# Attention and MLP on one core: weighed values in place of bias rows, batch 0 in row strips, a new written-out order

## The chip, the cores and the metric

One core of a Trainium2 chip runs the whole program. The metric is the time of one launch on the device, in microseconds (us); lower is better. The engines are named as the profile names them: PE (TensorE, matmuls), PEld (its weight loads), DVE (VectorE), ACT (ScalarE), POOL (GpSimd), SP (SyncE, which only issues DMAs here). DMAs issued from POOL go by the queue q0 (software descriptors, and only this queue can change the type on the way); DMAs issued from SP go by q1 and the one from ACT by q10 (hardware descriptors). All of them end on the same 16 DMA engines.

## What is computed

```python
B, H, S, D = 8, 8, 576, 64                  # batches, heads, tokens, head width
scores = q @ k.T / sqrt(D)                  # causal
cum    = cumsum(max(s, 0), axis=-1)         # the gate's running sum
scores = scores + min(cum[key] - cum[query], 0)
attn   = softmax(scores)                    # over the keys up to the query
x      = concat_heads(attn @ v)             # (8, 576, 512)
xn     = (x - mean) / sqrt(var + 1e-6) * g_ln
out    = x + max(xn @ w_ch1, 0) @ w_ch2     # 512 -> 2048 -> 512
```

All inputs and the output are float32 in device memory. Within a row of the softmax the query's own term of the gate cancels, so what matters of the gate is a factor exp(cum[key]) on each key. There are two ways to bring it in: as a term of the score (a bias), or as a factor on the key's row of v and on the one that counts for the softmax's denominator.

## The kernel before, in words

576 tokens are four tiles of 128 and a last one of 64. Each batch needs its k and q with the head width on the partitions (a transpose), scores with keys on the partitions, exp on ACT, the product with v on PE (for each head and query tile, `exp(scores)` is the stationary operand and v the moving one, with a column of ones for the denominator), a normalisation on DVE, the layer norm (DVE, with one power on POOL), and the MLP: 16 groups of hidden units (`mlp1`, four matmuls of 512 columns each, then a relu on ACT or DVE) and four token tiles of output (`mlp2`, 16 matmuls of 512 columns each, then an add on DVE and a DMA to memory). The 64-token ends of the batches are gathered two by two in a ninth, mixed MLP chunk.

Three kinds of batches are treated differently before the change:

- Batch 0 goes token tile by token tile, so that the work can begin when the first 128 tokens have landed. `ld_cast_tile` (L178) loads k and q of a tile with a change to bf16 on the way. The gate is put in as four bias rows: the running sum is scanned on DVE (`cum_scan`, L291), split into three bf16 pieces on DVE and ACT, transposed on PE (`bias_tr`, L271) and copied beside k and q, so that each head has 68 rows. `tile_tr` (L943) transposes every head by itself (8 transposes for each tile and group of four heads), `tile_scores` (L965) makes the scores of one head at a time from 68 rows, with a mask matmul (`L978`) on each diagonal block, and `tile_pv` (L1016) multiplies with v.
- Batch 1 uses bias rows too. Its k and q come pair of heads by pair (`ld_cast`, L181), where a partition holds six tokens of a head in a row, are transposed with `tr_kind` (L317), and go head by head through `scores` (L382), `scores_d` (L420), `pv` (L573) and `pv_norm` (L592).
- Batches 2 to 7 have no bias. POOL multiplies v and the ones with the weights exp(...) (`weigh_v` L229, `weigh_ones` L239). Two heads lie on the two halves of the partitions (64 rows each), and one `burst` (L541) sends the matmuls of both alternately to the two halves of the array. Six exps (`burst_exp`), four masks on POOL (`burst_mask`), then `pv_two` (L613) and `norm_two` (L639) for each head, `tails` (L514) for the last 64 keys of all heads. Batch 2's k and q come pair by pair like batch 1's, are copied on ACT (`side_two` L342), transposed on PE (`tr_two` L355) and copied back (`evac_two` L365). Batches 3 to 7 come as f32 rows by SP (`ld_rows` L211), are cast on POOL (`cast_rows`) and transposed by DMA (`tr_rows` L221).

The order of the work on every engine is written out by hand as words in a string, `PLAN` (L1278), and each word calls one function (`STEPS`, L1195). Each engine takes its instructions strictly in that order. The words used below are: `S`, `x`, `V`, `N` for scores, exp, product with v and normalisation of a tile of batch 0; `M` and `r` for pieces of batch 0's `mlp1` and their relu; `B2.n`, `bx`, `bm`, `Y`, `K` for burst, exp, mask, product and normalisation of the pair n (four pairs to a batch, so `B2.8` is the first burst of batch 2); `sd` for the tails; `u` and `U` for the next unit of the MLP queue, which holds the batches in turn; `vm` and `vo` for the weighing; `lr`, `lv` for f32 loads by SP; `la` and `l` for the layer norm's output and `D`, `Da` for its transpose by DMA.

POOL issues the loads that change the type among its other work. SP issues its DMAs in order, and a DMA of SP that waits for a buffer or for a result holds up those behind it.

Of the kernel before, what the change touches and what calls it, by code (L numbers as in the profile page):

```python
# [9 lines left out]
F32 = mybir.dt.float32  # L10
# [6 lines left out]
P = 128  # L17
# [13 lines left out]
def fast_path(  # L31
# [24 lines left out]
    KA = D + 4  # L56
# [5 lines left out]
    NOLD = 2  # L62
    NPAIR = 3
    N0 = 12
    D2 = D + 2
    ET = H * TL + 2 * TL
    NM = 10
    KT = 96
    QT = 6
    QP = S // QT  # L70

# [7 lines left out]
    early = ctx.enter_context(ExitStack())  # L79
    pairs = early.enter_context(tc.tile_pool(name="pairs", bufs=4))  # L80
    ps = ctx.enter_context(ExitStack())
    pool = {
        tag: ps.enter_context(
            tc.tile_pool(name="ps_" + tag, bufs=n, space=bass.MemoryType.PSUM)
        )
        for tag, n in (("m", 2), ("s", 3), ("t", 2), ("o", 1))
# [18 lines left out]
    eight = hT[0:BH, 0, 0 : 2 * P].bitcast(F32)  # L105
# [5 lines left out]

    def home(gam):
        return 2 if gam == 2 else gam % 2
# [11 lines left out]
    c3f = const.tile([P, 3 * S], BF16, name="c3")  # L125
    c3 = c3f[0:KT].rearrange("p (j s) -> p j s", j=3)
    ed = [c3f[:, i * ET : (i + 1) * ET] for i in range(2)]
    c_hi, c_mid, c_lo = (c3[0:BH, j, :] for j in range(3))
    zeros = hT[:, 1, :]

    rowb = const.tile([P, NT, 2 * H, KA], BF16, name="rowb")

    rows = [
        x[:, 0 : NT * 2 * H * D].rearrange("p (t u h d) -> p t u h d", t=NT, u=2, h=H)
        for x in (rowb.rearrange("p t h c -> p (t h c)"), kqf[2])
    ]

# [10 lines left out]
    ready = {}  # L148


    def pair_src(kind, g):
        src = k if kind == "k" else q
        b, j = g // 4, g % 4
        return src[b, 2 * j : 2 * j + 2].rearrange("h (p t) d -> p h (t d)", t=QT)

    def pair_tile(kind):
        return pairs.tile([P, 2, QT * D], BF16, name=kind + "p", tag=kind + "p")


    def tile_src(kind, t):  # L160
        pn = P if t < NF else TL
        src = k if kind == "k" else q
        return src[0, :, t * P : t * P + pn, :].rearrange("h s d -> s h d")

    def tile_dst(kind, t):
        pn = P if t < NF else TL
        u = "kq".index(kind)
        return rowb[0:pn, t, u * H : (u + 1) * H, 0:D]

    def ld_tile(kind, t, eng):  # L170
        tmp = stage.tile([P, H, D], F32, name="tiletmp", tag="st")
        eng.dma_start(out=tmp, in_=tile_src(kind, t))
        loaded[kind, t] = tmp

    def cast_tile(kind, t, eng):
        copy_on(eng, tile_dst(kind, t), loaded.pop((kind, t)))

    def ld_cast_tile(kind, t):  # L178
        nc.gpsimd.dma_start(out=tile_dst(kind, t), in_=tile_src(kind, t))  # L179
# [5 lines left out]
    def ld_cast_pair(g):  # L185
        ld_cast("k", g)
        ld_cast("q", g)

    def ld_cast_v(b, t):
        pn = P if t < NF else TL  # L190
        nc.gpsimd.dma_start(  # L191
            out=v_bf[b % 2][:pn, t, :, 0:D],
            in_=v[b, :, t * P : t * P + pn, :].rearrange("h s d -> s h d"),
        )
# [4 lines left out]
    src_of = {"k": k, "q": q, "v": v}  # L199

    def ld_f32(kind, b, t):
        pn = pn_of(t)
        own = kind == "v" and "v" in pool
        tmp = (pool["v"] if own else stage).tile([P, H, D], F32, name="rowtmp", tag="st")
# [4 lines left out]
        loaded[kind, b, t] = tmp  # L209

# [4 lines left out]
    def cast_rows(b, t, u):  # L215
        pn = pn_of(t)
        nc.gpsimd.tensor_copy(  # L217
            out=rows[b % 2][0:pn, t, u], in_=loaded.pop(("kq"[u], b, t))[0:pn]
        )
# [1356 lines left out]
```

## Time and profile before

| | us |
|---|---|
| three runs | 346.12, 345.09, 346.25 (median 346.12) |
| the profiled execution | 345.24 |
| its span, first to last instruction | 343.7 |
| PE busy | 333.9 (97%) |
| DVE busy | 207.1 (60%) |
| ACT busy | 186.8 (54%) |
| POOL busy | 168.7 (49%) |

The span of the profile runs from the first to the last instruction; 1.54 us of the execution's time lie around it. "Busy" is the time in which at least one instruction of the engine was under way. A matmul is under way far longer than it holds up the next one, so the price of a matmul on PE is read from start to start and not from its duration. A row of the timeline gives the start, the length, the engine, the line of the kernel, what is written and read, and how many neighbours of the same kind were merged into the row; in square brackets stands how long the engine had been idle before, and who released it. A row of a table by windows gives the stretch, its length, the busy time of PE, PEld, DVE, ACT and POOL with the number of instructions, the granted clock, the share of the DMA engines and GB/s. A row of a DMA queue gives the packets, MB (as written), and the time of the packets as a share of the 16 engines; the shares can pass 100% because packets of one engine overlap.

### The profile page before, as it was taken

The page shows a single profiled execution, that of the slowest core. Times are in us where ns is not written, and L with a number is a line of the kernel's source. Part 1 is how long each engine was busy: PE and PEld are TensorE (multiplying, and loading weights), DVE is VectorE, ACT ScalarE, POOL GpSimd, SP SyncE. Part 2 cuts the span into 40 slices and gives each one's busy share as a digit, 9 for nine tenths or more (in the row PEclk, how much of TensorE's full clock was granted, in tenths as well). Part 3 has the DMA queues.
Part 4 walks back from the last instruction along what each step waited for, and adds up shares of the span by engine and source line. Part 5 has one row for each costly group of instructions (what it writes and reads, how often), then busy time and mean ns, then how long its engine had stood idle before and what let it go on. Part 6 is the DMA issues. An engine that isn't in the chain of part 4 may idle for free.

```text
span 343.7 us, 8035 instructions
## 1 busy us (share of the span) xinstructions
PE 333.9 (97%) x3093; PEld 185.4 (54%) x3093; DVE 207.1 (60%) x589; ACT 186.8 (54%) x347; POOL 168.7 (49%) x306
## 2 busy tenths in 40 slices
PE   7999999899999999999999999999999999999994
PEld 2989765445545555555455555554555444444443
DVE  7688787937675787545753774557448624523412
ACT  4888899668755685448546864386344204202200
POOL 8997678876588766755684476441301001000000
PEclk9999999999999999999999999999999999999998
DMA  9999999799999999997687955600410141021022
GB/s 153 189 184 179 201 198 212 174 243 225 198 220 248 220 226 202 212 229 157 154 198 194 224 106 126 138 2 2 122 63 0 29 126 46 2 79 44 0 64 65
DMA packets 147962, 48.59 MB, mean 141 GB/s; under 512 B 135280, under 2 KB 143760, under 8 KB 147920
## 3 DMA queue, kind: packets, MB, share of 16 engines
q1 hardware_dynamic: 121856, 38.34, 51.4%
q0 software_dynamic: 24304, 8.92, 22.1%
q10 hardware_dynamic: 1760, 0.79, 0.9%
q8 instruction: 25, 0.41, 0.5%
q14 instruction: 17, 0.14, 0.1%
HBM read 37.11 MB, written 9.44 MB: 135 GB/s over the span
## 4 chain that ended last, share of the span: by engine, by line
PE 85%; POOL 7%; DVE 2%; DMA 2%; issue 1%; POOLq 0%
PE py L780 35%; PE ph L761 34%; PE pot L627 7%; DMA v_bf<-in_v_dram 2%; POOL v_bf L191 2%; PE sa L548 2%; POOL rowb L179 2%; PE sc L548 1%; PE sb L548 1%; PE pot L583 1%; DVE xn L710 1%; POOL w_bf L252 1%; POOL kq L910 1%; DVE yo L792 0%; DVE stats L669 0%
## 5 line engine op out<-in xcount | busy, mean ns | idle before, releaser
L780 PE MATMUL py<-w_bf,hT 128*128 128x512 bf16 (+2 forms) x608 | 130.9, 368 | 1.1 <-DVE yo L792 1.1
L761 PE MATMUL ph<-xT,w_bf 128*128 128x512 bf16 x480 | 109.8, 379 | 0.0
L752 ACT ACTIVATE hT<-ph 128x512 bf16<-128x512 f32 x102 | 61.2, 604 | 80.4 <-PE ph L761 78.8
L780 PEld LDWEIGHTS <-hT 128*128 128x128 bf16 x608 | 56.0, 98 | 61.4 <-issue 1.4
L761 PEld LDWEIGHTS <-w_bf 128*128 128x128 bf16 x544 | 51.0, 98 | 56.2
L492 POOL TENSOR_SCALAR_AFFINE_SELECT er<-er 128x256 bf16<-128x256 bf16 x96 | 37.5, 405 | 60.2 <-ACT er L553 45.1
L792 DVE SCALAR_TENSOR_TENSOR yo<-py,rstd,xb 128x512 f32<-128x512 f32 x32 | 24.0, 750 | 47.5 <-PE py L780 43.8
L553 ACT ACTIVATE er<-sb 128x512 bf16<-128x512 f32 x48 | 28.2, 609 | 21.7 <-PE sb L548 18.5
L750 DVE TENSOR_SCALAR hT<-ph 128x512 bf16<-128x512 f32 x34 | 23.4, 690 | 25.3 <-PE ph L761 24.6
L553 ACT ACTIVATE er<-sa 128x512 bf16<-128x512 f32 x48 | 28.6, 609 | 13.1 <-PE sa L548 10.2
L232 POOL TENSOR_TENSOR v_bf<-rowtmp,wt 128x512 bf16<-128x512 f32 (+1 forms) x30 | 33.8, 1134 | 2.8 <-DMA rowtmp<-in_v_dram 2.7
L553 ACT ACTIVATE er<-sc 128x512 bf16<-128x512 f32 x48 | 28.8, 613 | 5.4 <-PE sc L548 5.4
L627 PEld LDWEIGHTS <-er 128*128 128x128 bf16 x672 | 25.7, 97 | 9.5 <-issue 0.6
L627 PE MATMUL pot<-v_bf,er 128*128 128x66 bf16 x672 | 28.0, 193 | 0.0
L710 DVE SCALAR_TENSOR_TENSOR xn<-xb,mv,gb 128x512 bf16<-128x512 f32 x28 | 26.9, 960 | 1.0
L684 POOL TENSOR_TENSOR rstd<-rstd,mhalf 128x4 f32<-128x4 f32 (+1 forms) x8 | 8.8, 1094 | 36.9 <-DVE rstd L683 32.6
L644 DVE TENSOR_REDUCE sums<-pot 128x5 f32<-128x10 f32 x48 | 7.9, 165 | 30.0 <-PE pot L627 29.7
L669 DVE BATCH_NORM_STATS2 stats<-xb 128x6 f32<-128x128 f32 (+1 forms) x84 | 24.0, 323 | 0.4
L217 POOL CAST kq<-rowtmp 128x512 bf16<-128x512 f32 (+1 forms) x30 | 20.0, 681 | 6.3 <-DMA rowtmp<-in_k_dram 6.2
L647 DVE TENSOR_TENSOR xb<-pot,rinvs 128x256 f32<-128x256 f32 x48 | 20.4, 424 | 1.6
L548 PEld LDWEIGHTS <-kq 64*128 64x128 bf16 x360 | 11.2, 94 | 10.1 <-issue 4.7
L987 ACT ACTIVATE er<-st 128x512 bf16<-128x512 f32 x24 | 13.1, 603 | 1.8 <-PE st L978 1.8
(173 smaller groups left out, 398.3 us busy)
## 6 DMA issues: line engine op xcount, KB each, us to landing
out_dram<-yo SPq DMA_DIRECT2D x32, 256.0 KB
rowtmp<-in_v_dram SPq DMA_DIRECT2D x24, 256.0 KB
rowtmp<-in_k_dram SPq DMA_DIRECT2D x20, 256.0 KB
rowtmp<-in_q_dram SPq DMA_DIRECT2D x20, 256.0 KB
w_bf<-in_moe_w_ch_dram POOLq DMA_DIRECT2D x8, 512.0 KB, 9.2
kp<-in_k_dram POOLq DMA_DIRECT2D x8, 144.0 KB, 8.9
qp<-in_q_dram POOLq DMA_DIRECT2D x8, 144.0 KB, 8.9
v_bf<-in_v_dram POOLq DMA_DIRECT2D x8, 128.0 KB, 8.0
```

The costliest lines, as they stand in the source:

```text
L232: e.tensor_tensor(out=v_bf[b % 2][0:pn, t, :, 0:D], in0=loaded.pop(("v", b, t))[0:pn], in1=wt[0:pn, t, b, :].unsqueeze(2).to_broadcast([pn ...
L492: nc.gpsimd.affine_select(out=out, in_=out, compare_op=ALU.is_ge, fill=0.0, base=0, pattern=pattern, channel_multiplier=-1,)
L548: nc.tensor.matmul(a, lhsT=lhsT, rhs=rhs, start=True, stop=True)
L553: nc.scalar.activation(out=er[:, 2 * n % 4 + i, o : o + 512], in_=bank["B", n].pop((name, i)), func=ACT.Exp, scale=scale,)
L627: nc.tensor.matmul(pot[:, t, :], lhsT=cols, rhs=v_bf[b % 2][:, kb, h, :], start=(kb == 0), stop=(kb == t),)
L669: nc.vector.bn_stats(out=st[b][:, t, part, :], in_=x_tiles(b)[t][:, lo:hi])
L710: nc.vector.scalar_tensor_tensor(out=xn, in0=tiles[t], scalar=mvs[b][:, t, 0:1] if b > 0 else mean0[:, t : t + 1], in1=gb, op0=ALU.subtrac ...
L750: nc.vector.tensor_scalar_max(out=dst, in0=ph, scalar1=0.0)
L752: nc.scalar.activation(out=dst, in_=ph, func=ACT.Relu)
L761: nc.tensor.matmul(ph, lhsT=w1_bf[:, kd, fb * P : (fb + 1) * P], rhs=xT[:, :, kd, :], start=(kd == 0), stop=(kd == KD - 1),)
L780: nc.tensor.matmul(py[t], lhsT=hT[:, fb, t * P : (t + 1) * P], rhs=w2_bf[:, fb, c0:c1], start=(fb == 0), stop=(fb == FB - 1),)
L792: nc.vector.scalar_tensor_tensor(out=yo, in0=py[t], scalar=rs, in1=x[:, c0:c1], op0=ALU.mult, op1=ALU.add)
```

## The change

1. The bias rows go, and with them everything that makes them: the three pieces, their transposes and copies, the small DMAs of `aug`, the memsets of constant rows. All eight batches weigh v and the ones, so batches 0 and 1 need the weights first: load of the whole gate, relu, two scans, `wr`, `wT`, `wx` now stand at the start of the plan, and v of batches 0 and 1 comes as f32 by SP and is weighed on DVE or POOL.
2. k and q of batches 0, 1 and 2 come token tile by token tile in bf16 (`ld_cast_rows`: one run of 64 values for each token and head), are transposed two heads at a time on PE (`rows_tr`, eight transposes for each tile of a batch) and copied once (`rows_evac`). The loads pair by pair, `side_two`, `tr_two`, `evac_two`, `tr_kind`, `evac_half` are gone.
3. Batch 0's scores go in row strips: two heads alternate on the two halves of the array, and one mask matmul covers several diagonal blocks of a bank.
4. Batch 1 goes by bursts like the batches after it, with masks on POOL and tails.
5. All of batch 0's `mlp1` goes in pieces of one token tile (`M`, 16 pieces of 16 matmuls of 128 columns; before, eight pieces and eight units of 512 columns). Its `mlp2` goes in named quarters `Z.t.q`.
6. PSUM: four banks for scores and two for transposes at first, six for scores after `to`.
7. The plan is new from its start to about the middle and shifted a little behind that; memsets and loads that stood ahead of it are words of it now.

The core of the diff:

```diff
-    def ld_cast(kind, g):
-        ready[kind, g] = pair_tile(kind)
-        nc.gpsimd.dma_start(out=ready[kind, g][0:QP], in_=pair_src(kind, g))
+    def ld_cast_rows(b, t, u):
+        pn = pn_of(t)
+        nc.gpsimd.dma_start(
+            out=rows_of(b)[0:pn, t, u],
+            in_=(k, q)[u][b, :, t * P : t * P + pn, :].rearrange("h s d -> s h d"),
+        )
+
+    def rows_tr(b, t):
+        pn = pn_of(t)
+        tr = ptile("s" if new[0] else "t", [P, 2, NJ, P], "trp", BF16)
+        for u in range(2):
+            for j in range(NJ):
+                nc.tensor.transpose(
+                    tr[:, u, j, 0:pn],
+                    rows_of(b)[0:pn, t, u, 2 * j : 2 * j + 2].rearrange("p h d -> p (h d)"),
+                    ident[0:pn, 0:pn],
+                )
+        bank["P", b, t] = tr
...
-    def tile_scores(t, g, i):
-        a = ptile("s", [P, 512], "st")
-        for c in range(4 if t < NF else 8):
...
+    def tile_scores(t, c):
+        w = pn_of(t)
+        n = 512 // w
+        banks = [ptile("s", [P, 512], f"st{i}") for i in range(2)]
+        blocks = [divmod(n * c + x, min(t + 1, NF)) for x in range(n)]
+        diag = [x for x in range(n) if blocks[x][1] == t]
+        for i in range(2):
+            if diag:
+                nc.tensor.matmul(
+                    banks[i].rearrange("p (x s) -> p x s", s=w)[:, diag[0] :: t + 1],
+                    lhsT=ident,
+                    rhs=maskT.unsqueeze(1).to_broadcast([P, len(diag), P]),
+                    start=True,
+                    stop=False,
+                )
+        for x in diag + [x for x in range(n) if x not in diag]:
+            j, kb = blocks[x]
+            for i in range(2):
+                nc.tensor.matmul(
+                    banks[i][:, x * w : (x + 1) * w],
+                    lhsT=k_pair(0, j, i, kb),
+                    rhs=kq_flat(0)[i * D : (i + 1) * D, 1, j, t * P : t * P + w],
+                    start=x not in diag,
+                    stop=x not in diag[:-1],
+                )
...
+        sums = small.tile([P, G], F32, name="sums0", tag="sums")
+        nc.vector.tensor_reduce(out=sums[0:pn], in_=pot[0:pn, :, D:D2], axis=AX.X, op=ALU.add)
+        nc.vector.reciprocal(out=rinv, in_=sums[0:pn])
...
-        "s": lambda n: scores(n // H, n % H),
-        "v": lambda n: pv(n // H, n % H),
+        "Z": first_out,
+        "lk": ld_cast_rows,
+        "P": rows_tr,
+        "p": lambda b, t, eng: rows_evac(b, t, eng),
```

The start of the new plan, and the stretch around batch 2's first burst (`lt.u.t` and `lk.b.t.u` load k or q, u = 0 or 1, of a tile; `P.b.t` and `p.b.t` are its transposes and their copy; `me`, `vz`, `mk`, `ez`, `kz`, `id` are memsets, the mask and the identity on POOL):

```
relu W.1 ck:D lv.0.0 me vz.0 one W.2 mk ez cq:A scan.0 kz id idf scan.1 P.0.0 wr vz.1 lt.0.1 lt.1.1
pk.0.0:A pq.0.0:A wT S.0.0 wx vm.0.0:D lt.0.2 P.0.1 lt.1.2 p.0.1:D lt.0.4 lt.0.3 lt.1.3 P.0.2 gb rv
x.0.0.1 vo.0:P x.0.0.0 V.0.1 w1.0 S.1.0 p.0.2:D S.1.1 lv.0.2 V.0.0 w1.1 N.0.1 lv.0.1 P.0.3 N.0.0 x.1.0.0
...
Y.6.1 p.2.1:A P.2.0 ga.1.0.3 K.6.1 sd.2 ga.1.1.0 Z.3.0 vo.2:P bm.7.1 Y.7.1 P.2.2 ga.1.1.2 ga.1.1.1
vm.2.4:P lv.2.2 Z.3.1 bm.7.2 bx.7.2 K.7.1 bx.7.0 lr.3.1 p.2.3:A p.2.0:A se.2 bm.7.0 p.2.2:D Y.7.0
ga.1.0.2 qu.6 B2.8 ga.1.0.4 vm.2.0:P K.7.0 bx.8.3 bx.8.1 ga.1.2.0 ga.1.2.3 qu.7 ga.1.0.1 Z.3.2 Z.2.0
vm.2.1:P vm.2.3:P l.0 bm.8.1 bx.8.0 bx.8.2 lr.3.2 ga.1.1.3 ga.1.2.2 bx.8.4 ga.1.2.1 vm.2.2:P Z.3.3 B2.9
bx.8.5 l.1 l.3 Z.2.1 lr.3.0 l.2 bx.9.3 Z.2.2 La.4 bx.9.4 D lv.3.0 bx.9.5 sm.2 bm.8.0 bm.8.2 bx.9.1 Z.2.3
```

More of the change, by code (lines that the diff above doesn't have):

```diff
@@ L420, in scores_d @@
[L420 to L448 removed]
+    def kq_flat(b):
+        return kq[2 if b == 1 else b % 2]
@@ L1005, in last_scores, with last_exp @@
             )
-            nc.tensor.matmul(a[:, c], lhsT=ident, rhs=maskT[:, 0:TL], start=False, stop=True)
-        bank["Sk"] = a
-    def last_exp():
-        nc.scalar.activation(out=er_slot(7), in_=bank.pop("Sk"), func=ACT.Exp, scale=scale)
+        for j in range(NJ):
+            for i in range(2):
+                r = slice(i * D, (i + 1) * D)
+                nc.tensor.matmul(
+                    banks[i][0:TL, j * TL : (j + 1) * TL],
+                    lhsT=kq_flat(0)[r, 0, j, NF * P : S],
+                    rhs=kq_flat(0)[r, 1, j, NF * P : S],
+                    start=False,
+                    stop=j == NJ - 1,
+                )
+        for i in range(2):
+            bank["Sk", i] = banks[i]
+    def last_exp(i):
+        two = ed_rows(0).rearrange("p (j i) c -> p i j c", i=2)
+        nc.scalar.activation(
+            out=two[:, i],
+            in_=bank.pop(("Sk", i))[0:TL, 0 : NJ * TL].rearrange("p (j c) -> p j c", c=TL),
+            func=ACT.Exp,
+            scale=scale,
+        )
     xb[0] = xpool.tile([P, NF, Dm], F32, name="xb", tag="xb")
```

677 lines of the change are left out of this document (184 added, 493 removed).

## The prediction

> **What bounds the kernel now.** I read the page's shares first, then the chain that ended last, then the table by windows cut at the one place that matters here, the first burst of batch 2.
>
> ```profile
> span 343.7 us, 8035 instructions
> PE 333.9 (97%) x3093; PEld 185.4 (54%) x3093; DVE 207.1 (60%) x589; ACT 186.8 (54%) x347; POOL 168.7 (49%) x306
> ...
> DMA  9999999799999999997687955600410141021022
> ```
>
> PE is busy 97% of the span, and the DMA engines are full for the first half of it. Both can be the bound early, so the chain decides.
>
> ```profile
> 24.60 3.39 POOL v_bf L191 x4
> 27.98 8.25 DMA v_bf<-in_v_dram
> 36.70 0.86 PE ph L761 x4
> ```
>
> Up to 36 us the chain is loads: POOL issues them and PE waits for what lands. Behind that it is PE. The burst of batch 2 (`B2.8`) starts here:
>
> ```profile
> 69.64 0.39 PE L548 MATMUL sa<-kq 64*128 64x512 bf16 x2
> ```
>
> ```profile
> 0.00:69.64 69.64, 64.80 (x891) 47.50 (x892) 54.84 (x154) 55.29 (x102) 56.86 (x100) 1.00 1.38 187
> 69.64:343.70 274.06, 269.09 (x2204) 137.93 (x2203) 152.28 (x435) 131.50 (x245) 111.89 (x207) 1.00 0.59 130
> 320.00:343.70 23.70, 18.81 (x120) 10.06 (x118) 7.25 (x15) 0.60 (x1) 0.00 (x0) 0.95 0.19 47
> ```
>
> The columns behind the length are busy us of PE, PEld, DVE, ACT, POOL. Ahead of 69.64 PE is idle 69.64 - 64.80 = 4.84 us. Behind it the idle time is 274.06 - 269.09 = 4.97 us, and 23.70 - 18.81 = 4.89 of that is the end of the program. So from `B2.8` on PE runs without a gap to its end; what the change does to the time is **when `B2.8` starts, and how much PE work is left then**. All that the diff changes in substance stands ahead of it.
>
> **The PE work.** Prices are start to start.
>
> ```profile
> 10.62 1.09 PE L948 MATMUL trt<-ident,rowb 128*68 128x128 bf16 x16
> 20.69 0.39 PE L970 MATMUL st<-kq 68*128 68x128 bf16 x4
> 20.91 0.22 PE L978 MATMUL st<-maskT,ident 128*128 128x128 bf16 x1
> 20.97 0.53 PE L1028 MATMUL pot<-v_bf,er 128*128 128x65 bf16 x12
> ...
> 40.62 0.42 PE L322 MATMUL trqk<-ident,qp 96*128 96x96 bf16 x6
> 40.88 0.38 PE L390 MATMUL sa<-kq 68*128 68x512 bf16 x1
> ...
> 42.94 0.38 PE L390 MATMUL sa<-kq 68*128 68x512 bf16 x1
> ...
> 43.59 0.60 PE L761 MATMUL ph<-xT,w_bf 128*128 128x512 bf16 x2
> ...
> 71.64 2.75 PE L780 MATMUL py<-w_bf,hT 128*128 128x512 bf16 x12
> 74.33 0.39 PE L548 MATMUL sa<-kq 64*128 64x512 bf16 x2
> ...
> 75.08 0.59 PE L627 MATMUL pot<-v_bf,er 128*128 128x66 bf16 x14
> ...
> 75.55 0.59 PE L627 MATMUL pot<-v_bf,er 128*128 128x66 bf16 x14
> ```
>
> A transpose of 128 columns: (1.09 - 0.22) / 15 = 0.058. A score or mask of 128 columns: 0.28 / 5 = 0.056. A transpose of 96: 0.26 / 6 = 0.043. A head of batch 1: 43.59 - 42.94 = 0.65. A unit of 4 matmuls of 512 columns: (74.33 - 71.64) / 3 = 0.90, of which a little is the switch; 0.86 in the chain's row above. A burst of two heads: 75.08 - 74.33 = 0.75, which is why strips pay: two heads for little more than one. One head's product with v: 0.47, so 0.031 for each of 15. A matmul of 64 columns I take at 0.03, by the 66-column row.
>
> Removed: batch 0's 80 transposes (64 x 0.058 + 16 x 0.043 = 4.4), 15 transposes of the bias (0.65), its scores and masks (112 of 128 columns, 48 of 64: 7.7); batch 1's 48 transposes (2.1), eight heads of scores with their ten masks and tails (5.2 + 0.8), its products (3.7); batch 2's 48 transposes (2.1). Sum 26.65. Added: three batches of 32 + 8 transposes (3 x (32 x 0.058 + 8 x 0.03) = 6.3); batch 0's scores in pairs (40 x 0.056 + 16 x 0.03 = 2.7) with the same mask columns in fewer matmuls (1.9); batch 1's bursts, tails, products (3.0 + 0.25 + 3.8); `mlp1` all in pieces, 128 x 0.058 for 8 x 0.86 (+0.5). Sum 18.45. The saving is **8.2 us of PE**. Moved: at `B2.8` the new plan has six quarters `Z` of batch 0 left where the old one had four units, and `sd.2` is done where it was not: 2 x 0.86 - 0.25 = 1.5 more is left behind `B2.8`. Behind it I find nothing else that PE does for more or less.
>
> So PE alone would reach `B2.8` at 69.64 - 8.2 - 1.5 = 59.9, if it idled as much as before.
>
> **The DMA work.** All loads share the 16 engines; I price each kind in a stretch that it fills almost alone. The rows are of q0 from 10 to 13 us (casts of 64 values, 128 bytes written), from 37 to 39 (weights), from 40 to 41.5 (mostly pair loads), and of q1 from 72 to 74 (f32 rows).
>
> ```profile
> q0 software_dynamic: 3678, 0.46, 242.8%
> ...
> q0 software_dynamic: 408, 0.41, 124.3%
> ...
> q0 software_dynamic: 392, 0.29, 125.9%
> ...
> q1 hardware_dynamic: 2028, 0.51, 112.6%
> ```
>
> A tile of 128 tokens and 8 heads is 1024 packets: 1024 / (3678 / 3) = 0.84 us by q0, 1024 / (2028 / 2) = 1.01 as f32 by q1. A slice of weights is 512 packets: 512 / 200 = 2.56, with some 8 of the 408 taken for semaphores. A pair load is 192 packets at about 240 a us: 0.80.
>
> Before, up to the last pair load: 16 tiles by q0 (batch 0's k and q 7, two batches of v 9) 13.4, 16 pair loads 12.8, 8 slices 20.5, `gb` 0.7, and about 9 f32 tiles that ran beside them 9.1: 56.5. They were through here (q0 from 61 to 62, then 62 to 64):
>
> ```profile
> q0 software_dynamic: 24, 0.02, 10.4%
> ...
> q0 software_dynamic: 2, 0.00, 0.3%
> ```
>
> The first packets ran at about 2 us, so 56.5 us of work took 59.5: the engines were full, with 5% lost. From landing to `B2.8` it took another 8 us, since the side copy on ACT, six transposes and a copy stood in the order behind other things.
>
> After, up to the last tile of batch 2's k and q (`lk.2.2.1`): 25 tiles by q0 20.9, slices 20.5, `gb` 0.7, k0, q0 and two batches of v as f32, 11 x 1.01 = 11.1. That is 53.2. Batch 2's v and batch 3's first rows by SP, 8.5 tiles or 8.6, come late in the same stretch and share it. With 5% lost, 2 us of start and 0.7, an estimate, for a gap between the last tile of batch 0 and the first slice (POOL weighs the ones between them): 53.2 x 1.05 + 2.7 = **58.6** if none of those 8.6 gets in ahead, 61.8 x 1.05 + 2.7 = **67.6** if all of it does. Which it is hangs on SP: those loads stand behind the output of `Z.0.3`, which needs the last slice of `mlp2`'s weights, so they start as the last 7.5 us of q0's work begin. How two queues share is shown by the stretch from 5 to 9 us:
>
> ```profile
> q0 software_dynamic: 1988, 0.25, 97.2%
> q1 hardware_dynamic: 1825, 0.50, 69.5%
> ```
>
> Packet for packet, nearly. So the 7.5 us would be stretched by somewhat over half of the 8.6: **63.5**. Then `P.2.2`, its copy and `B2.8`: 8 x 0.058, a copy of 0.7 as in the row below, and the latencies, 1.5 together. `B2.8` at **65.0**.
>
> ```profile
> 11.89 0.68 DVE L142 COPY kq<-trt 68x1024 bf16<-68x1024 bf16 x1
> 67.08 2.22 SPq L732 DMA_TRANSPOSE xT<-xn  x1
> ...
> 79.26 8.68 SPq L224 DMA_TRANSPOSE kq<-kq  x3
> ...
> 89.60 0.84 POOL L144 COPY kz<-kq 64x256 bf16<-64x256 bf16 x2 [0.49 <-DMA kq<-kq]
> ```
>
> The small-packet rule weighed: the Trainium skill, "DMA: Bandwidth & Descriptors", section "Why small descriptors are slow (HBM only)", gives a 256-byte descriptor 11 cycles where its bytes need 8. By it I estimate 1.375 for the token tiles against 51 / 48 = 1.06 for the 1536-byte runs of the pair loads, so 6.4 us for a batch's k and q would become 8.3. The rows say 7.5 (9 x 0.84 for 8 x 0.80), and I keep the rows; by the page the time would be 1.5 us later.
>
> **Other parts.**
>
> ```profile
> 19.67 0.53 POOL L915 MEMSET er<- 128x512 bf16 x1
> ...
> 20.44 1.01 POOL L919 MEMSET v_bf<- 64x528 bf16 x2
> ...
> 38.39 0.60 POOL L934 MEMSET kz<- 128x576 bf16 x1
> ...
> 58.37 1.19 POOL L1239 MEMSET c<- 128x640 bf16 x2
> ```
>
> The new start puts these 3.3 us of POOL's memsets, the mask and the identity ahead of the first cast load, but k, q and v of tile 0 and v's next tiles come by SP and ACT meanwhile and fill the engines; cover gone, it costs the same 0.7 gap again. ACT and DVE lose the pieces, the copies of `side_two` and half of the copies of batches 1 and 2 and gain eight weighings and twelve reductions; both had about 15 us free ahead of 69.64, so I cost it at nothing. Behind `B2.8` the next thing that could be late is `xT` of batch 1: its layer norm now ends some 6.5 us behind `B2.8` (the order has seven statistics, four `l`, one output ahead of `D`), then 2.2 us of issue and about 1.6 to land, as the last transposes of batch 3 did (their issue over at 79.26 + 8.68 = 87.94, the copy to `kz` released at 89.60). That is 10.5; PE has 6 Z, 3 bursts, 5 products until its first `u`, 5.2 + 2.3 + 2.4 = 9.9, plus exps to wait for. I take nothing, and 2.5 us as the upper bound if SP's queue is full of rows.
>
> **Sum.** 345.24 (the profiled execution) + (65.0 - 69.64) + 1.5 = **342.1**. The median of the runs shown is 346.12, 0.9 above that execution, inside their spread. A measurement of this kernel tells about 0.5% (1.7 us) from no change, so faster means below 344.4.
>
> **Rivals.** (1) *PE sets the pace.* Batch 3's rows do not get in ahead, the last tile lands near 58.6, and `B2.8` starts when PE gets there, 59.9 to 60.5: 345.24 - 8.2 = 337.0. For it: PE's idle time ahead of `B2.8` was only 4.84 us; against it: the 5% are already tight. (2) *Slower: the loads decide outright.* All of the f32 rows interleave, the last tile lands at 67.6 or later, `B2.8` starts at 69.1, and `D` queues behind the rows of batch 3 on SP for the 2.5 us: 345.24 - 0.5 + 1.5 + 2.5 = 348.7. It decides against the change from `B2.8` at about 70. For it: nine tiles of 1024 packets for eight loads of 192 in each of two batches; against: nobody needs batch 3's rows so early and only SP's order puts them there. (3) *No change*, between the two: `B2.8` at 67 to 69, 344 to 347. (4) *The strips do not overlap* in batch 0, since full-height masks stand between them: 2.7 us more on PE, hidden under the loads in the forecast case, 339.7 in rival 1. The bursts' 0.39 us for two matmuls speak against it.
>
> **Numbers.** Forecast case, 339 to 344.4: 0.42. PE's pace, 334 to 339: 0.24. No change: 0.20. Slower: 0.14. Faster is 0.66. The range leaves out little below PE's pace with half of its old idle time gone (337.0 - 2.4 = 334.6) and ends at the slower case: 335 to 348.5.
>
> **What would show it.** PE busy falls from 333.9 to about 326. The last cast packets of q0 run at 63 to 64, with q1 beside them from about 52. PE's largest waits are in front of the transposes of batch 2 (`trp` released by DMA), and `B2.8` comes within about 2 us of the last landing. From there to the end PE has no gap but a short one at the first MLP unit of batch 1. Wrong if PE waits more for exps, masks or weights of v than for loads ahead of `B2.8`, if the fifth burst starts before 61 or after 69, or if a gap opens behind it.

## The result, and the profile after

The changed kernel takes **364.95 us** (median of 362.56, 365.02, 367.49 and 364.89) against 346.13 for the kernel before beside it: ratio 1.0552, 95% interval 1.0478 to 1.0626. It is slower by 18.8 us, where a gain of about 3 us (342.1 us) was forecast. The profiled execution is the fastest of the four, 362.56; its span is 17.4 us longer than that of before. In a few of the runs below an execution came out 1.5% or more above the fastest of its kernel and is called slow; the ratios leave these out, the medians do not.

The page of the changed kernel, the rows that answer to those of before, and the granted clock in 40 slices of 9 us:

```profile
span 361.1 us, 7970 instructions
...
PE 332.9 (92%) x3064; PEld 183.1 (51%) x3090; DVE 198.9 (55%) x586; ACT 172.9 (48%) x320; POOL 170.5 (47%) x307
...
PEclk9898999699999999999999999999999999999998
DMA  9999899996899999999979995450040041011022
```

PE is busy as long as before (333.9), but 92% of the span and not 97%, and its clock is no longer full: slices 2, 4 and 8 show a 6 or an 8. The DMA row shows an 8 in slice 5 (36 to 45 us) and a 6 in slice 10 (81 to 90 us), inside the stretch that loads should fill. Where the time went is read from one table by windows, cut at 43 us, at `B2.8` (79.19 here, 69.64 before) and at `B2.16`, the first burst of batch 4; first the kernel before:

```profile
0.00:43.00 43.00, 39.45 (x635) 32.73 (x636) 33.20 (x104) 34.10 (x63) 35.65 (x60) 1.00 1.57 181
43.00:69.64 26.64, 25.35 (x259) 14.77 (x257) 21.64 (x51) 21.19 (x40) 21.20 (x41) 1.00 1.07 195
69.64:122.20 52.56, 52.48 (x531) 27.99 (x531) 34.68 (x101) 35.44 (x68) 39.36 (x72) 1.00 1.06 221
122.20:343.70 221.50, 216.61 (x1677) 109.94 (x1674) 117.60 (x334) 96.06 (x178) 72.53 (x136) 0.99 0.48 108
```

and the changed kernel:

```profile
0.00:43.00 43.00, 34.05 (x501) 24.76 (x502) 24.63 (x75) 22.06 (x41) 26.91 (x45) 0.92 1.44 167
43.00:79.19 36.19, 28.67 (x388) 19.95 (x388) 19.43 (x59) 19.12 (x33) 25.39 (x48) 0.91 1.22 163
79.19:139.34 60.15, 54.70 (x526) 28.53 (x531) 38.89 (x118) 36.50 (x69) 44.23 (x81) 1.00 0.97 200
139.34:361.10 221.76, 215.50 (x1658) 109.90 (x1674) 115.94 (x336) 95.22 (x178) 73.92 (x136) 0.99 0.49 111
```

Length less PE busy is PE's idle time: 3.55, 1.29, 0.08 and 4.89 before, 8.95, 7.52, 5.45 and 6.26 after. That is 18.4 us more idle for 1.0 us less busy, the whole 17.4. Behind `B2.16` the two kernels are alike; all of the loss lies ahead of it, in three stretches of about equal weight (5.4, 6.2 and 5.4 us of added idle time).

POOL, DVE and PE in the changed kernel, first POOL (start, length, engine, line, what is written and read; in brackets how long the engine stood idle before, and who released it):

```profile
32.46 0.77 POOL L237 DMA_DIRECT2D w_bf<-in_moe_w_ch_dram  x1
42.30 1.04 POOL L214 TENSOR_TENSOR v_bf<-rowtmp,wt 128x512 bf16<-128x512 f32 x1 [9.07 <-DMA rowtmp<-in_v_dram]
...
45.12 2.30 POOL L237 DMA_DIRECT2D w_bf<-in_moe_w_ch_dram  x3
47.39 2.48 POOL L168 DMA_DIRECT2D rowb<-in_k_dram  x3
...
63.35 1.04 POOL L453 TENSOR_TENSOR rstd<-rstd,mhalf 128x4 f32<-128x4 f32 x1 [7.04 <-DVE rstd L452]
64.38 1.49 POOL L300 TENSOR_SCALAR_AFFINE_SELECT er<-er 128x256 bf16<-128x256 bf16 x4
...
68.36 0.89 POOL L168 DMA_DIRECT2D rowb<-in_q_dram  x1
```

DVE:

```profile
60.14 1.28 DVE L214 TENSOR_TENSOR v_bf<-rowtmp,wt 128x512 bf16<-128x512 f32 x2 [8.96 <-DMA rowtmp<-in_v_dram]
```

and PE:

```profile
9.25 0.52 PE L847 MATMUL trw<-identf,hT 64*128 64x64 f32 x5 [1.78 <-DVE hT L834]
...
30.48 2.74 PE L791 MATMUL ph<-xT,w_bf 128*128 128x128 bf16 x24 [3.07 <-DMA w_bf<-in_moe_w_ch_dram]
...
65.57 0.95 PE L396 MATMUL pot<-v_bf,er 128*128 128x66 bf16 x14 [5.52 <-POOL er L300]
...
79.19 0.39 PE L356 MATMUL sa<-kq 64*128 64x512 bf16 x2
```

Both engines stand on the weighing of a tile of batch 1's v (L214) whose f32 load has not landed. Behind POOL's wait of 9.07 us stand the issues of three slices of weights and all loads of batch 2; while it waits, the DMA engines run dry:

```profile
40.00:42.00 2.00, 1.81 (x42) 1.70 (x40) 1.61 (x5) 1.24 (x3) 0.00 (x0) 1.00 0.37 76
42.00:44.00 2.00, 2.00 (x45) 2.00 (x42) 1.86 (x8) 0.00 (x0) 1.62 (x4) 1.00 0.03 8
```

Behind DVE's wait of 8.96 us stands the variance of batch 0; POOL waits 7.04 for that, and behind POOL stand the masks for batch 1's first product, on which PE waits 5.52 us, and the last load of batch 2's q, issued at 68.36. Its last packets run at 74 to 78 us, not at 63 to 64; the rows of q0 from 74 to 76 and from 76 to 78 us:

```profile
q0 software_dynamic: 271, 0.03, 26.6%
...
q0 software_dynamic: 12, 0.00, 1.1%
```

Why v is late is on SP. Its loads of v run in one row to 52 us, since only two buffers take them and each load waits for the weighing of the tile two before it:

```profile
2.20 49.89 SPq L160 DMA_DIRECT2D rowtmp<-in_v_dram  x10
```

The clock is the second part. Three stretches run at half speed, each behind a wait:

```profile
30.50:33.50 3.00, 3.00 (x26) 2.64 (x26) 0.67 (x2) 0.00 (x0) 2.50 (x3) 0.50 1.54 193
9.50:13.00 3.50, 3.23 (x27) 1.73 (x26) 1.39 (x2) 1.52 (x3) 3.38 (x7) 0.51 2.19 139
64.00:65.50 1.50, 0.00 (x0) 0.00 (x0) 1.06 (x2) 0.00 (x0) 1.50 (x5) 0.57 1.63 104
65.50:71.00 5.50, 5.27 (x74) 4.00 (x75) 2.89 (x11) 2.74 (x6) 5.22 (x11) 0.50 1.03 167
```

The clock of the third fell already in the wait, at about 64.2 us. Half of their busy time, (3.00 + 3.23 + 5.27) / 2 = 5.75 us, is the slow clock. So `B2.8` at 79.19 is 62.73 - 5.75 = 57.0 us of work, 5.75 of slow clock and 16.5 of idle time; before it was 64.8 of work and 4.8 of idle time. Whether the slow clock cost any time is another question (experiment 5).

### The profile page after: what moved, and what is told of

It reads as the page before. It is cut to its first block, busy times and chain, and to the rows that moved or that the text cites. A ratio compares the mean times of both kernels' runs of the same rounds, so it can differ in the third digit from the quotient of the medians.

```text
span 361.1 us, 7970 instructions
## 1 busy us (share of the span) xinstructions
PE 332.9 (92%) x3064; PEld 183.1 (51%) x3090; DVE 198.9 (55%) x586; ACT 172.9 (48%) x320; POOL 170.5 (47%) x307
## 4 chain that ended last, share of the span: by engine, by line
PE 71%; DMA 10%; POOL 9%; DVE 5%; issue 2%; SPq 1%; ACT 0%; POOLq 0%
PE py L549 29%; PE ph L530 27%; PE pot L396 6%; DMA rowtmp<-in_v_dram 4%; DMA w_bf<-in_moe_w_ch_dram 3%; POOL rowb L168 2%; DMA rowtmp<-in_q_dram 2%; PE ph L791 2%; PE sa L356 2%; PE sb L356 1%; PE sc L356 1%; POOL er L300 1%; DVE xn L479 1%; POOL v_bf L214 1%; DMA kq<-kq 1%
## 5 line engine op out<-in xcount | busy, mean ns | idle before, releaser
L530 PE MATMUL ph<-xT,w_bf 128*128 128x512 bf16 x448 | 101.6, 379 | 0.4 <-DMA xT<-xn 0.4
L521 ACT ACTIVATE hT<-ph 128x512 bf16<-128x512 f32 x97 | 58.0, 603 | 86.6 <-PE ph L530 85.5
L300 POOL TENSOR_SCALAR_AFFINE_SELECT er<-er 128x256 bf16<-128x256 bf16 x112 | 46.4, 432 | 45.3 <-ACT er L361 28.7
L361 ACT ACTIVATE er<-sa 128x512 bf16<-128x512 f32 x56 | 33.4, 610 | 26.6 <-PE sa L356 24.8
L361 ACT ACTIVATE er<-sb 128x512 bf16<-128x512 f32 x56 | 33.5, 606 | 23.4 <-PE sb L356 21.7
L396 PE MATMUL pot<-v_bf,er 128*128 128x66 bf16 x784 | 34.1, 196 | 10.0 <-POOL er L300 7.6
L396 PEld LDWEIGHTS <-er 128*128 128x128 bf16 x784 | 30.9, 99 | 22.2 <-POOL er L300 11.9
L214 POOL TENSOR_TENSOR v_bf<-rowtmp,wt 128x512 bf16<-128x512 f32 (+1 forms) x32 | 33.6, 1058 | 10.4 <-DMA rowtmp<-in_v_dram 10.2
L361 ACT ACTIVATE er<-sc 128x512 bf16<-128x512 f32 x56 | 33.4, 612 | 5.3 <-PE sc L356 2.8
L416 DVE TENSOR_TENSOR xb<-pot,rinvs 128x256 f32<-128x256 f32 x56 | 23.8, 425 | 1.9
L791 PE MATMUL ph<-xT,w_bf 128*128 128x128 bf16 x256 | 18.4, 228 | 3.8 <-DMA w_bf<-in_moe_w_ch_dram 3.5
## 6 DMA issues: line engine op xcount, KB each, us to landing
rowb<-in_k_dram POOLq DMA_DIRECT2D x7, 128.0 KB, 10.5
```

The costliest lines, as they stand in the source:

```text
L214: e.tensor_tensor(out=v_bf[b % 2][0:pn, t, :, 0:D], in0=loaded.pop(("v", b, t))[0:pn], in1=wt[0:pn, t, b, :].unsqueeze(2).to_broadcast([pn ...
L300: nc.gpsimd.affine_select(out=out, in_=out, compare_op=ALU.is_ge, fill=0.0, base=0, pattern=pattern, channel_multiplier=-1,)
L361: nc.scalar.activation(out=er[:, 2 * n % 4 + i, o : o + 512], in_=bank["B", n].pop((name, i)), func=ACT.Exp, scale=scale,)
L396: nc.tensor.matmul(pot[:, t, :], lhsT=cols, rhs=v_bf[b % 2][:, kb, h, :], start=(kb == 0), stop=(kb == t),)
L416: nc.vector.tensor_tensor(out=xb[b][:, :, hs], in0=pot[:, 0:NF, 0:D], in1=rinv[:, 0:NF].unsqueeze(2).to_broadcast([P, NF, D]), op=ALU.mult,)
L521: nc.scalar.activation(out=dst, in_=ph, func=ACT.Relu)
```

## The experiments

Theory W: the loss is waits in order for tiles of v. Rivals: the volume of the loads (D), the later start of the cast loads (S), later also the clock (C) and SP's own order (Q). Each run below stands beside runs of the kernel before on the same chip, and the ratios are to those. The medians of different groups come from different chips (345.1 to 346.4 for the kernel before), so between groups the ratios are the better measure.

**1. Eight buffers for batch 1's v.** The pool of f32 rows, empty at that time, takes them.

```diff
-        own = pool["v"] if kind == "v" and (b, t) != (0, 0) else stage
+        own = pool["v"] if kind == "v" and b != 1 and (b, t) != (0, 0) else stage
```

> Theory W (waits for v): batch 1's f32 tiles of v are issued late because SP has two buffers for them, and POOL and DVE stand in order on their weighing. With eight buffers for them SP issues all five by about 20 us; POOL's wait of 9.07 us at 42.30 and DVE's of 8.96 us at 60.14 go (under 1 us each), the hole in the DMA engines from 41 to 46 us goes, the last cast packet of q0 comes at 66 to 68 instead of 76, B2.8 at about 70, and the time is 349 to 356. Rival D (volume: the loads as such take the engines that long): 4.5 tiles more in the full stretch from 20 to 35 us push the slices of weights back by as much, the last cast packet stays within 2 us of 76, and the time stays 361 to 367. Rival S (start: the first cast load 3.8 us later than before): nothing changes ahead of 10 us, so 361 to 367 too.

358.24 us, ratio 1.0388 (1.0294 to 1.0482): by the ratios 5.7 us of the 18.8 came back (6.7 by the medians), less than expected, and the two intervals just touch. The profiles show it more sharply: POOL and DVE wait for v no more, the hole is gone, the last cast packets run at 64 to 66 us, and `B2.8` came at 73.51, 5.7 us sooner. But that is still 8 us behind the last packets: PE had become late itself, by waits for slices of w_ch1 at 30.9 and 41.0. W is right, and too small.

**2 to 4. The order on POOL, on DVE, and all three.** POOL's weighing moved behind the issues that it held up; DVE's three moved behind the variance; both with the buffers.

```diff
-... w2.0 P.1.0 vm.1.0:P ... vo.1:P ... tk.1 ... w2.3 ... lk.2.4.1 ... ec
+... w2.0 P.1.0 ... w2.3 ... lk.2.4.1 ... vm.1.0:P vo.1:P tk.1 ec
-A.3 vm.1.3:D ... vm.1.4:D A.1 vm.1.2:D Z.0.2 R ... Z.1.3
+A.3 ... A.1 Z.0.2 R ... Z.1.3 vm.1.3:D vm.1.4:D vm.1.2:D
```

> Only POOL's order: the weighing of batch 1's first tile of v stands behind the issues of the last weight slices and five loads of batch 2, not ahead of them. Theory W: the hole from 41 to 46 us is filled, but v's tiles still come by two buffers, so DVE's wait of 8.96 us at 60 stays within 2 us, and with it POOL's 7.04 us for the rstd; B2.8 comes 2 to 4 us sooner: 358 to 363. Rival D: the last cast packet comes no more than 2 us sooner, 362 to 367. Rival S: 361 to 367.

> Only DVE's order: the weighing of batch 1's last three tiles of v stands behind the variance of batch 0 and its statistics, not ahead of them. Theory W: POOL's wait of 7.04 us for the rstd and PE's of 5.5 us for the mask go; PE waits for the weighing itself instead, until about 64; B2.8 at 74 to 76: 357 to 362. Rival D: masks come sooner, the loads do not: B2.8 within 2 us of 79, 362 to 367. Rival S: 361 to 367.

> The edits of the three others together. Theory W: each takes away a part of the same chain, so not more than the largest of them by 3 us: 346 to 354, with no hole in the DMA engines ahead of the last cast packet, which comes at 64 to 67. Rival D: 361 to 367. Rival S: 361 to 367.

363.24 (1.0484, 1.0400 to 1.0567), 365.38 (1.0576, 1.0494 to 1.0658) and 362.42 (1.0459, 1.0379 to 1.0540). Neither order alone did anything that the scatter lets one see, and on top of the buffers both together look 4 us worse than the buffers alone, in intervals that overlap. All three came out above what W expected of them. In the run with DVE's order PE waited for the weighing instead, in the place of the mask, and further on for the last tile of q:

```profile
62.69 0.43 PE L396 MATMUL pot<-v_bf,er 128*128 128x66 bf16 x9 [2.72 <-DVE v_bf L214]
...
71.86 0.61 PE L178 MATMUL trp<-ident,rowb 128*128 128x128 bf16 x4 [1.95 <-DMA rowb<-in_q_dram]
```

A wait in order is not cured by moving the word that waits, as long as what it waits for is late.

**5. PE kept busy in its two longest waits** (changed kernel, idle matmuls only).

```diff
-X.2 M.2.0.0 ... Y.4.0
+X.2 W.14 M.2.0.0 ... W.22 Y.4.0
```

> The changed kernel with idle matmuls put into PE's two longest waits (14 of 512 columns ahead of the pieces that wait for the third slice of w_ch1, 22 ahead of batch 1's first product), nothing else. Theory C (clock): a wait of 3 us or more is followed by 3 to 6 us at half clock, so a wait costs its length and 1.6 to 2.7 us more; with PE kept busy the granted clock stays 1.00 at 30 to 34 and 64 to 71 us, and the time falls by 3 to 4.5 us: 359 to 362. Rival: PE has slack behind both waits (it waits for loads and masks again), so the clock costs nothing: 363 to 367.

364.34 us, 1.0532 (1.0455 to 1.0608): no gain that the intervals let one see. The clock did what C says, the time did not:

```profile
30.50:34.00 3.50, 2.94 (x32) 1.96 (x30) 1.11 (x2) 0.02 (x1) 2.50 (x3) 1.00 1.68 188
...
65.50:71.00 5.50, 2.95 (x64) 2.09 (x63) 3.52 (x11) 2.47 (x5) 5.48 (x12) 1.00 1.07 144
```

From 65.5 to 71 the clock is 1.00 and not 0.50, and PE is busy 2.95 us and not 5.27: the work is done faster and PE waits for the rest; `B2.8` starts at 79.56, no sooner than without. Half clock in these two stretches, where PE would have waited for loads and masks anyway, cost nothing.

**6 to 8. Three edits, each on top of the first.** Batch 1's v issued by ACT at 28 to 40 us instead of by SP at 20; three tiles of batch 3's rows ahead of the outputs on SP; five memsets of POOL behind the second slice of weights.

```diff
-        nc.sync.dma_start(
+        (nc.scalar if kind == "v" and b == 1 else nc.sync).dma_start(
...
-lr.3.1 ... lr.3.2 ... Z.3.3 ... lr.3.0 ... lr.3.3
+lr.3.1 lr.3.2 lr.3.0 lr.3.3 ... Z.3.3
...
-relu W.1 ck:D lv.0.0 me vz.0 one W.2 mk ez cq:A scan.0 kz id idf ... vz.1 lt.0.1 ... w1.1
+relu W.1 ck:D lv.0.0 id mk one W.2 cq:A scan.0 idf ... lt.0.1 ... w1.1 me vz.0 ez kz vz.1
```

> Batch 1's v with eight buffers as in the first experiment, but issued from ACT between its other work at 35 to 45 us, where the hole in the DMA engines was, and not by SP at 20 us. Theory W with the place of the loads: v of batch 1 no longer stands in the full stretch from 22 to 36, the third and fourth slices of w_ch1 land 2 to 4 us sooner than in the first experiment, and the hole is filled: B2.8 at 69 to 72, time 353 to 357 (that experiment: 358.24). Rival (the sum of loads is what counts, not their order): within 1.5 us of it, 357 to 360. Rival (issues on ACT delay exps): over 360.

> The first experiment, and three tiles of batch 3's rows moved on SP ahead of the outputs of batch 0's last tiles. Theory Q (SP's order): those loads stand behind outputs that wait for PE, the DMA engines stand idle from 76 to 80 us, and batch 3's transposes come late for B2.12; moved, the hole goes, the last transpose ends about 5 us sooner, and PE's idle time of some 5 us between B2.8 and B2.16 falls to 1 to 2: 353 to 356. Rival: the casts on POOL behind the masks set the transposes, not the loads: 357 to 360.

> The first experiment, with five memsets of POOL moved from ahead of the first cast load to behind the second slice of weights. Theory S (start): the first cast load is issued at about 2.3 us instead of 5.57, all that follows on q0 lands 2 to 3 us sooner, B2.8 at 70 to 71, 354 to 356. Rival (the engines are full from 2 us on with f32 tiles, so the casts only change places with them): 357 to 360.

357.48 (1.0315, 1.0225 to 1.0404), 354.50 (1.0248, 1.0175 to 1.0322) and 358.12 (1.0370, 1.0289 to 1.0451), against 358.24. Q is supported by the medians: with the rows the time is 3.7 us less, in intervals that overlap. The profile of that run, the slowest of its five, does not show the gain: PE's waits for batch 3's transposes, 0.7 us in experiment 1, are gone and `B2.12` starts 0.7 us sooner, but `B2.16` starts at 133.75 and not at 133.30. The place of v gave 1.9 us at `B2.8` (71.65) and no more than scatter at the end; the start gave 1.3 at `B2.8` (72.21) and nothing at the end, so S is out as the main cause. What took the gain back in the profile of the run with the rows is the next wait in order, behind `B2.12`: POOL casts a tile of batch 4 whose load has not landed, and a mask behind it holds PE. This wait was followed by half clock too (0.61 from 119 to 122 us), and here PE was busy throughout, so that it was not free.

```profile
116.45 0.61 POOL L199 CAST rowb<-rowtmp 128x512 bf16<-128x512 f32 x1 [4.16 <-DMA rowtmp<-in_q_dram]
117.01 0.77 POOL L300 TENSOR_SCALAR_AFFINE_SELECT er<-er 128x256 bf16<-128x256 bf16 x2
```

```profile
117.47 0.59 PE L396 MATMUL pot<-v_bf,er 128*128 128x66 bf16 x14 [2.57 <-POOL er L300]
```

**9 and 11. All that helped, and POOL's order on top.** Edits 1, 6, 7, 8 and the two casts of that tile moved behind three masks; then `vm.1.0:P vo.1:P tk.1` moved behind `w2.3`.

```diff
-bm.13.2 bx.13.2 bx.13.1 cr.4.2.1 bm.13.0 ... bm.13.3 cr.4.2.0 ... bm.13.1
+bm.13.2 bx.13.2 bx.13.1 bm.13.0 ... bm.13.3 ... bm.13.1 cr.4.2.1 cr.4.2.0
```

> The experiments that helped, together: batch 1's v from ACT into eight buffers, batch 3's rows ahead of the outputs, the memsets behind the weights, and two of batch 4's casts on POOL moved behind three masks of pair 13, since PE waited 2.57 us there for a mask behind a cast that waited 4.16 us for its load. Theory W and Q (in-order waits are what was lost): the parts add up, B2.8 at 70 to 71, B2.16 at 129 to 131, time 349 to 353. Rival L (with the waits gone the loads themselves bind): B2.8 stays at 71 to 73 and the time at 353 to 356.

> The combination with the weighing of batch 1's first tile and what follows it moved on POOL behind the last three slices of w_ch2. If POOL's order still matters: POOL's wait of about 5 us ahead of those issues goes, B2.8 1 to 2 us sooner than in the combination, 348 to 351. Rival L (loads bind): within 1.5 us of it.

351.40 us, 1.0155 (1.0095 to 1.0215), and 353.66, 1.0231 (1.0177 to 1.0286). The combination took back 13.5 of the 18.8 us, with `B2.8` at 70.28 as expected and `B2.16` at 128.62, a little ahead of the expected 129; POOL's order added nothing, against what was expected. It is the best version found, and it still loses to the kernel before.

```profile
0.00:43.00 43.00, 34.91 (x517) 25.60 (x518) 27.30 (x79) 22.38 (x41) 32.89 (x55) 0.92 1.51 178
43.00:70.28 27.28, 25.55 (x374) 17.60 (x372) 18.54 (x55) 19.02 (x33) 20.69 (x38) 1.00 1.45 198
70.28:128.62 58.34, 55.17 (x529) 28.73 (x530) 39.87 (x120) 36.83 (x69) 44.77 (x81) 1.00 1.01 204
```

The second stretch is healed: 27.28 us long, 1.73 idle, full clock. The first is not: 8.1 us idle at a clock of 0.92.

**10. Without the loads of batch 1's v** (changed kernel, a tile of k stands in, so batch 1's output is another).

```diff
+        keep.append(tmp)        (ld_tile, k of batch 0)
...
+        if kind == "v" and b == 1:
+            loaded[kind, b, t] = keep[0]
+            return
```

> The changed kernel without the loads of batch 1's v at all: their place is taken by a tile of batch 0's k that is in memory already, so the output of batch 1 is another. This takes the waits and the 4.5 tiles of loading away. Theory W: against the first experiment, which took away the waits and kept the loads, it gains at most what the loads cost, 4.5 us; against the changed kernel 8 to 12 us: 353 to 357, B2.8 at 68 to 71. Rival (the waits are not the cost): 358 or more.

353.38 us, 1.0160 (1.0102 to 1.0218): 11.6 less than the changed kernel by the medians. Against experiment 1, which has the loads and not the waits, it is 4.9 less by the medians, 7.9 by the ratios and 2.2 by the spans of the profiled pair (353.0, 355.2): the times do not say what the loads cost, which were priced at 4.5. The profiles separate the two. From batch 1's first burst, `B2.4`, to `B2.8`, in the changed kernel, in experiment 1 and here:

```profile
48.27:79.19 30.92, 23.42 (x288) 14.92 (x289) 15.91 (x48) 16.50 (x30) 20.33 (x38) 0.89 1.35 178
```

```profile
50.61:73.51 22.90, 21.07 (x288) 13.45 (x289) 16.09 (x48) 16.39 (x30) 17.12 (x33) 1.00 1.49 195
```

```profile
47.70:70.59 22.89, 21.17 (x290) 13.46 (x289) 15.98 (x48) 16.39 (x30) 17.12 (x33) 1.00 1.32 163
```

Without the waits this stretch is 8.0 us shorter, whether the loads are there or not. The loads, issued early in experiment 1, show ahead of it, where `B2.4` starts 2.9 us later than without them. In these profiles the waits cost more than the loads.

**12. Half of batch 2's k and q** on the combination (half of the heads are not loaded, so batch 2's output is another).

```diff
-            out=rows_of(b)[0:pn, t, u],
+            out=rows_of(b)[0:pn, t, u, 0 : H // (1 + b // 2)],
```

> The combination with only half of the heads of batch 2's k and q loaded (the other half keeps what is in the buffer, so batch 2's output is another): 3.8 us of loads less ahead of B2.8. Rival L (with the waits gone the loads bind): B2.8 comes 3 to 4 us sooner than in the combination and the time falls by 2.5 to 4 us. Theory W (order and waits still bind): less than 1.5 us.

1.0175 (1.0095 to 1.0254) against 1.0155, `B2.8` at 69.48 against 70.28: under 1 us, and all of it lies ahead of `B2.4` (46.59 against 47.39); the stretch from there to `B2.8` is 22.89 us in both. With the waits gone the late loads do not bind.

**13 to 16. The start, and the slices of w_ch1,** on the combination: eight idle matmuls in PE's wait for the gate's scans; the first scores ahead of that wait; then, with the eight, the third slice four loads sooner, and the fourth as well.

```diff
-pk.0.0:A pq.0.0:A wT S.0.0
+pk.0.0:A pq.0.0:A W.8 wT S.0.0        (13, 15, 16)
+pk.0.0:A pq.0.0:A W.6 S.0.0 wT        (14)
-lt.1.4 ... lk.1.1.1 ... lk.1.4.1 ... w1.2 ... lk.1.4.0 ... lk.1.0.0 ... w1.3
+lt.1.4 w1.2 ... lk.1.1.1 ... lk.1.4.1 ... lk.1.4.0 w1.3 ... lk.1.0.0        (16; 15 leaves w1.3)
```

> The combination, with eight idle matmuls of 512 columns (1.7 us) ahead of the transposes of the gate's weights, where PE waits 1.71 us for the scans and then runs at half clock from about 9.5 to 13 us. Theory C2 (with the waits for loads gone, the clock counts): granted clock 1.00 from 10 to 20 us instead of 0.66, B2.8 1.5 to 2.5 us sooner, 349 to 350.5. Rival (slack again, as when the two longest waits were filled in the changed kernel): within 1 us of 351.4.

> The same with six idle matmuls, and the first scores moved ahead of the transposes of the gate's weights, since they need no gate any more. If the order at the start counts on top of the clock: scores and exps of tile 0 start 0.5 to 1 us sooner, 348 to 350. Rival: within 1 us of 351.4.

> The combination with idle matmuls at the start, and the third slice of w_ch1 issued four loads earlier, since PE waits 2.10 us for it at 26.4 us and what was won ahead of it was given back there. Theory O (order of the first loads): the wait goes, B2.8 1 to 2 us sooner (69.72 there), 349 to 351. Rival: the tiles that it passes (batch 0's last and batch 1's first) land later and PE waits for them instead: 351 to 354.

> The same with the fourth slice moved ahead of four tiles of batch 1 as well. Theory O: up to 1 us more, 348 to 351. Rival: batch 1's transposes wait instead, 351 to 354.

352.88 (1.0188, 1.0138 to 1.0239), 351.56 (1.0152, 1.0110 to 1.0193), 353.30 (1.0200, 1.0166 to 1.0234) and 353.65 (1.0201, 1.0166 to 1.0236): nothing, where gains were expected. In run 13 the clock from 10 to 20 us is 1.00, and 0.66 in the combination. Most of what was won at the start is waited away at the third slice in run 13; with both slices ahead, run 16 waits for batch 1's tiles instead:

```profile
28.54 1.70 PE L791 MATMUL ph<-xT,w_bf 128*128 128x128 bf16 x21 [1.94 <-DMA w_bf<-in_moe_w_ch_dram]
```

```profile
36.57 0.94 PE L178 MATMUL trp<-ident,rowc 128*128 128x128 bf16 x8 [2.84 <-DMA rowc<-in_k_dram]
```

**17. Half of batch 1's k and q** on run 13 (the other half is zero, so batch 1's output is another).

```diff
+    nc.vector.memset(rows[1][:, :, :, H // 2 : H], 0.0)
...
-            out=rows_of(b)[0:pn, t, u],
+            out=rows_of(b)[0:pn, t, u, 0 : H // (1 + b % 2)],
```

> The combination with idle matmuls at the start, with only half of the heads of batch 1's k and q loaded (the other half is zero, so batch 1's output is another): 3.8 us of loads less, all of it ahead of 36 us. Theory E (the loads of the first 40 us set PE's pace there, whichever way they are ordered): batch 1's first burst at 43 to 45 instead of 46.83, B2.8 2 to 3 us sooner, 349.5 to 351 (352.88 there). Rival (PE waits for exps, relus and copies of its own chain): within 1 us, as with the half of batch 2's loads.

350.25 us, 1.0113 (1.0080 to 1.0146) against 1.0188. `B2.4` came at 44.60 instead of 46.83 and `B2.8` at 67.50 instead of 69.72, as theory E has it: of 3.8 us of loads taken out of the first 40 us, 2.2 came through to `B2.8`, all of it already at `B2.4`; the same amount taken out later changed nothing behind `B2.4`. In this profiled pair the 2.2 us were given back ahead of `B2.12` (98.54 against 98.66), where PE waited 2.00 us for `xT` of batch 1; the medians are 2.6 us apart, and the intervals just meet.

## Why the prediction was wrong

- **PE's work: the right sign, about half the size.** 8.2 us were to go, and 1.5 to move behind `B2.8`. In experiment 17, whose clock is full up to `B2.8`, PE is busy for 38.52 + 21.18 = 59.7 us ahead of it, 6.99 of them idle matmuls, for 64.80 and 5.71 before: 6.4 us less work where 9.7 was forecast. Behind it PE is busy for 271.88 us for 269.09, 2.8 more for 1.5. So some 4 us of PE's work went, not 8.2; which price or count was too high is not shown. (The changed kernel's own trace, worked out as above, gives 7.8 less and 1.1 more, but lacks the records of 24 matmuls behind `B2.8`: 2179 for 2203 weight loads.) The mark "PE busy falls to about 326" did not come: it reads 332.9 with the slow clock in it.
- **The step that failed: "the engines were full, with 5% lost", and `B2.8` at 65.0 from it.** The sum took loads as a row that runs as soon as the engines are free. Here they were issued by engines that stood in line for other loads: the hole at 40 to 46 us, the last casts at 68.36, the last landing at 76 instead of 63.5. The text held SP's loads back only by the output of `Z.0.3`; the two buffers of v, the buffer of a tile freed by a weighing, and that weighing standing in the middle of POOL's and DVE's order, were not followed. Experiment 1 shows 5.7 us of it at `B2.8`, and the stretch from `B2.4` to `B2.8` 8.0. The prediction's own row from 5 to 9 us spoke against the 5% as well: by its prices, 1988 and 1825 packets are 1.6 + 1.8 = 3.4 us of work in 4 us.
- **"I cost it at nothing" for DVE's eight weighings.** Their length (1.28 us for two in the row above) was set against some 15 us of free time. What counted was the landing that each waits for, and what is queued behind it: 8.96 us on DVE, 7.04 on POOL, 5.52 on PE.
- **"If it idled as much as before."** This was the hidden term. PE's saving lies mostly in the first 43 us, and there PE waited for loads: busy time fell from 39.45 to 34.05, and idle time rose from 3.55 to 8.95 (in a stretch of fixed length the one follows from the other), its longest wait being 3.07 us for a slice of weights. In the best version that stretch still has 8.1 us idle, while the one from 43 us to `B2.8` takes 27.28 us for 26.64 before. That the early loads set it is supported by experiments 13 to 17 and not proven by them: reordering moved the wait, and only fewer loads shortened the stretch clearly.
- **"From there to the end PE has no gap": wrong.** Between `B2.8` and `B2.16` PE idled 5.45 us. Not `xT` of batch 1 was late, for which 2.5 us had been set aside (0.38 us of wait; its three terms add up to 10.3 and not 10.5, which changes nothing). Some 3 us of the 5.45 are waits for the rows of batches 3 and 4, which stood behind outputs on SP and casts on POOL: 1.3 for batch 3's transposes, 2.0 for masks. With both edits, in experiment 9, 5.45 fell to 3.2.
- **The memsets: right.** They were put at nothing, or 0.7 us without cover; moving them gave 1.3 us at `B2.8` and nothing in the time (experiment 8).
- **The rivals.** The slower one had a chance of 0.14, and the right sign. Its mechanism, all f32 rows interleaving, was not what happened (SP issued batch 3's first rows at 74.08, behind the issue of the last cast at 68.36), and so its 348.7 was 16 us short. Of the marks set for a failure three came: ahead of `B2.8` PE waited more for masks and weights of v (6.4 us) than for loads (4.3), `B2.8` started after 69, and a gap opened behind it.

What stays open is the last 5 us of the combination: how much of them other orders of the first loads could win, and why PE has about 1.3 us more to do behind `B2.8` than was forecast.

## What to carry to other kernels

Before pricing an added operation by its length, ask what it waits for, how many buffers stand behind that load, and what is queued behind it on an engine that runs in order; above all on the engine that also issues the loads. PE work saved in a stretch whose pace the loads set is no time saved, and a wait taken away there tends to come back at the next load. A wait moved in the order is still a wait: here more buffers helped, and an earlier issue where the loads had room; another place for the waiting instruction alone did not.

## What the runs showed of the hardware

The granted clock of PE fell to half in or behind waits and stayed there for 3 to 7 us, as the rows above show. The length of one wait does not decide it. The wait of 2.84 us in run 16, ahead of 36.57 us, was followed by half clock (0.50 from 38 to 40 us), and so was one of 1.78 us ahead of 9.25 us in the changed kernel, though PE had made little but transposes around it. In experiment 1 a wait of 2.89 us, ahead of 41.01 us, was followed by full clock:

```profile
41.01 0.84 PE L791 MATMUL ph<-xT,w_bf 128*128 128x128 bf16 x12 [2.89 <-DMA w_bf<-in_moe_w_ch_dram]
```

```profile
41.00:45.00 4.00, 3.19 (x64) 3.03 (x65) 1.34 (x4) 1.19 (x2) 1.32 (x2) 1.00 1.76 162
```

The Trainium skill, "TensorE: Matmul & The Clock Gate", Part 1, gives a free-running window of about 3.4 us in which PE's activity is watched, and half clock after at least one idle window. The stretches of 3.0 and 3.5 us are near one such window and the third, from 64.2 to 71.0, near two; but here waits shorter than a window were enough, and the measurement decides. Such a stretch was free where PE would have waited anyway (experiment 5), and not where PE had work throughout (the run with the rows, from 119 to 122 us).

Two queues side by side moved less than their prices add up to. In experiment 1, from 26 to 28 us:

```profile
q0 software_dynamic: 737, 0.15, 82.2%
q1 hardware_dynamic: 728, 0.18, 69.1%
```

Of these 1465 packets 62 are larger than 512 bytes, those of a slice of weights. Priced as the prediction does, that is 675 / 1226 + 62 / 200 + 728 / 1014 = 0.55 + 0.31 + 0.72 = 1.6 us of work in 2 us, with the engines shown as busy. Whether the mix is slower or POOL had too few casts queued, since it waited for an earlier load's landing twice around that time, is open.
